# Retention and a multiplicative FFN on one core: weights converted 1024 columns at a time, w3 transposed by VectorE

## The chip, the cores and the metric

One core of a Trainium2 chip runs the whole program. The metric is the device time of one execution in microseconds (us). Short names: PE is TensorE (PEld its weight loads), DVE is VectorE, ACT is ScalarE, POOL is GpSimd, SP is the queue of SyncE, which issues most DMAs.

## What is computed

A retention block (8 batches, 8 heads, 576 positions, head size 64) gives x, which a feed-forward block takes. The weights arrive as 64-bit floats.

```python
scores = scale * np.matmul(q, k.transpose(0, 1, 3, 2))
ret = scores * Dmat[None, :, :, :]       # gamma[h] ** (i - j) for i >= j, else 0
x = np.matmul(ret, v)                    # then (B,H,S,D) -> (B*S, H*D) = (4608, 512)
a = x @ w1                               # 512 -> 1024
b = x @ w2                               # 512 -> 1024
h = a * b @ w3                           # 1024 -> 1024
out = h @ w_out                          # 1024 -> 512
```

## The kernel before, in words

**Chunks and units.** Tokens are taken in 4 pairs of batches. The retention runs in chunks of 128 positions (`load`, `scale`, `front`, `score`, `state`, `pv`): `load` fetches q, k and v from SP's queue, `front` transposes q and k on PE, `score` and `pv` are products, `state` carries the state along. The FFN works on a pair of batches and a third of the sequence: `up(i, n, fp)` makes one quarter fp of the 1024 inner columns of a and b by a Strassen scheme of seven products (L493), and multiplies a and b (L519). `down` multiplies by the matrix W = w3 @ w_out, which is made once on the chip.

**One `up`, in order.** Five PSUM tiles serve seven products; p1 and p5 are used twice. ACT copies p1 to c (L506), DVE adds S2 x T2 (the first addition, L498), S3 x T3 (the second), p5 = S1 x T1 (the third), A22 x -T4 (the fourth); then PE adds A12 x B21 to p1, ACT copies p1 again (L513), PE adds S4 x B22 to p5 (the seventh product; in the profile it is the group xT,wS), DVE adds p5 (the fifth addition) and multiplies the two halves of c (L519). There is one c. After each addition `convert(conv)` moves the conversion of the weights on by `conv` steps. The pool `acc` has seven PSUM banks.

**Conversion of the weights.** A 64-bit weight comes as two 32-bit words. Per block, DVE takes the exponent from the high word (tile e, L362) and the mantissa in two instructions (tile m, L366 and L369); ACT turns the exponent into a scale by two relus on e (L372, L373); DVE puts the sign on it (L383, the last reader of the loaded block) and multiplies m and e into the weight (L392, the output). `conversion()` is a generator: each `yield` is a step, and whoever calls `convert(n)` runs n steps, so the order of all engines is the order in which the program calls it. Between `begin_block` (L362 to L373) and `end_block` (L383, L392) of one block stands `begin_block` of the next. w1 and w2 come as four quarters, each of two matrices and two row halves: 16 blocks; when a quarter is whole, `strassen_weights` makes its sums S1 to S4 (L156). w_out is 8 blocks, w3 16, two for each 128 rows. A block is 512 columns, 512 KB as loaded; five buffers hold loaded blocks, so the load of block n+5 is issued when block n is done (L395, L396). DVE's transposes in 32x32 blocks are used elsewhere (`front_blocks`, L198).

**w3 @ w_out.** `w3_tr` transposes 128 rows of w3 on PE in eight 128x128 transposes (L438), and ACT copies them out of PSUM (L440). `w3_mm` multiplies them by w_out (L448; in the profile each product is two records) and ACT stores the sum (L451). The loop at L730 first runs the six `up`s of `todo`; with each it goes on with the conversion, and it interleaves `w3_tr` and `w3_mm`. When `todo` is empty, it runs `convert(10)` and PE has only this work until all 8 groups of rows are done. After it come one `up`, one `down` and the rest of retention and FFN.

**Memory.** The pools `raw` (loaded blocks, e, m) and the attention's pools share the right side of SBUF; `wst` (w_out, w3 and its transpose) takes the attention's place after L714. `open_attention` at L761 takes the place of `raw`, so the loads of the second half wait for the last block.

Of the kernel before, what the change touches and what calls it, by code (L numbers as in the profile page):

```python
# [8 lines left out]
F32 = mybir.dt.float32  # L9
I32 = mybir.dt.int32  # L10
U32 = mybir.dt.uint32
ALU = mybir.AluOpType
PSUM = bass.MemoryType.PSUM

# [24 lines left out]
def kernel(  # L39
# [13 lines left out]
    nc = tc.nc  # L53
    moe_w1, moe_w2, moe_w3, moe_w_out = (
        w.bitcast(I32).rearrange("r (c t) -> r c t", t=2) for w in (moe_w1, moe_w2, moe_w3, moe_w_out))
    B, H, S, D = q.shape
    DM = H * D
    DF = moe_w3.shape[0]
    CV = 512
    P = 128  # L60
    NP = H // 2
# [11 lines left out]
    KD = DM // P  # L73
    KF = DF // P
    QC = CV // 2
    NQ = DF // QC
    heads = [slice(j * D, (j + 1) * D) for j in range(2)]
# [10 lines left out]
    pools = {}  # L88
# [52 lines left out]

    halves = range(DF // CV)
    wA = [wp.tile([P, 2, KD, CV], F32, tag=f"wA{h}", name="wA") for h in halves]
# [10 lines left out]
    def strassen_weights(fp):  # L154
        def tt(out, in0, in1, op):
            nc.vector.tensor_tensor(out=A(fp, out), in0=A(fp, in0), in1=A(fp, in1), op=op)  # L156

        tt("S1", "A21", "A22", ALU.add)
        tt("S2", "S1", "A11", ALU.subtract)
        yield  # L160
        tt("S3", "A11", "A21", ALU.subtract)
        tt("S4", "A12", "S2", ALU.subtract)
        live["S", fp] = True
        yield

    BL = 32
# [142 lines left out]
    blocks = []  # L309
    for fp in range(NQ):  # L310
        for j, w in enumerate((moe_w1, moe_w2)):
            for r in range(2):
                blocks.append((("w12", fp, j, r), w))
    blocks += [(("wo", g), moe_w_out) for g in range(KF)]
    blocks += [(("w3", ft, g0), moe_w3) for ft in range(KF) for g0 in range(0, DF, CV)]
    at = {key: n for n, (key, _) in enumerate(blocks)}
    loaded, begun, converted, turned = [0], [0], [0], [0]

    def load_block():
        n = loaded[0]  # L320
        if n == len(blocks):
            return
        key, w = blocks[n]
        t = raw.tile([P, CV, 2], I32, tag="raw", name="raw", bufs=5)
        if key[0] == "w12":
            _, fp, _, r = key
            src = w[2 * r * P:2 * (r + 1) * P, fp * QC:(fp + 1) * QC, :]
            t2 = t.rearrange("p (c n) t -> p c n t", c=2)
            if r == 0:
                nc.sync.dma_start(t2, src.rearrange("(c p) n t -> p c n t", p=P))  # L330
            else:
                for half in range(2):
                    nc.sync.dma_start(t2[heads[half]],
                                      src.rearrange("(c a d) n t -> a d c n t", a=2, d=D)[1 - half])
        else:
            r, c0 = (key[1], 0) if key[0] == "wo" else key[1:]
            nc.sync.dma_start(t, w[r * P:(r + 1) * P, c0:c0 + CV, :])
        live["raw", n] = t
        loaded[0] += 1

    def converted_to(n):
        key, _ = blocks[n]
        if key[0] == "w12":
            _, fp, j, r = key
            return wA[fp // 2][:, j, 2 * r:2 * r + 2, fp % 2 * QC:fp % 2 * QC + QC]
        if key[0] == "wo":
            return live["wo"][:, key[1], :]
        _, ft, g0 = key
        if ("w3", ft) not in live:
            live["w3", ft] = pools["wst"].tile([P, DF], F32, tag="w3", name="w3")  # L350
        return live["w3", ft][:, g0:g0 + CV]

    def begin_block():
        n = begun[0]
        t = live["raw", n]
        lo, hi = t[:, :, 0], t[:, :, 1]
        e = raw.tile([P, CV], I32, tag="exp", name="e")
        m = raw.tile([P, CV], I32, tag="man", name="m")
        vec = nc.vector


        vec.tensor_scalar(out=e, in0=hi, scalar1=1, scalar2=21,  # L362
                          op0=ALU.logical_shift_left, op1=ALU.logical_shift_right)
        yield

        vec.tensor_scalar(out=m, in0=hi, scalar1=0x000FFFFF, scalar2=0x00100000,  # L366
                          op0=ALU.bitwise_and, op1=ALU.bitwise_or)
        yield
        vec.scalar_tensor_tensor(m.bitcast(F32), in0=lo.bitcast(U32), scalar=2.0 ** -32, in1=m,  # L369
                                 op0=ALU.mult, op1=ALU.add)  # L370
        relu = mybir.ActivationFunctionType.Relu
        nc.scalar.activation(e, e, relu, bias=lim[:, 0:1], scale=-1.0)  # L372
        nc.scalar.activation(e, e, relu, bias=lim[:, 1:2], scale=-2.0 ** 23)  # L373
        live["em", n] = e, m
        begun[0] += 1
        yield

    def end_block():
        n = converted[0]
        hi = live["raw", n][:, :, 1]  # L380
        e, m = live["em", n]
        vec = nc.vector
        vec.scalar_tensor_tensor(e, in0=hi, scalar=-(1 << 31), in1=e,  # L383
                                 op0=ALU.bitwise_and, op1=ALU.bitwise_or)
        yield
        key = blocks[n][0]
        while not (key[0] == "w12" or "wo" in live and (key[0] == "wo" or key[1] < turned[0] + 2)):
            yield "wait"
        out, m, e = converted_to(n), m.bitcast(F32), e.bitcast(F32)
        if key[0] == "w12":  # L390
            m, e = (x.rearrange("p (c n) -> p c n", c=2) for x in (m, e))
        vec.scalar_tensor_tensor(out, in0=m, scalar=2.0 ** -20, in1=e, op0=ALU.mult, op1=ALU.mult)  # L392
        converted[0] += 1

        if n >= 4:  # L395
            load_block()  # L396
        if key[0] == "w12" and key[1] > 0 and key[2:] == (1, 1):
            yield from strassen_weights(key[1])
        yield

    def conversion():


        yield from begin_block()
        while converted[0] < len(blocks):
            if begun[0] < len(blocks) and converted[0] not in (1, 2, 3):
                yield from begin_block()
            yield from end_block()
            if begun[0] == converted[0] < len(blocks):
                yield from begin_block()  # L410
# [11 lines left out]
    def convert(n):  # L422

        for _ in range(n):
            if go_on() is not None:
                return

    def convert_up_to(n):
        while converted[0] < n:
            assert go_on() is None  # L430


    def w3_tr(ft):
        t = pools["wst"].tile([P, KF, P], F32, tag="w3T", name="w3T")
        for i in range(0, KF, NP):
            tp = acc.tile([P, NP, P], F32, tag="acc", name="tp")
            for n in range(NP):
                nc.tensor.transpose(tp[:, n, :], live["w3", ft][:, (i + n) * P:(i + n + 1) * P],  # L438
                                    ident)
            nc.scalar.copy(t[:, i:i + NP, :], tp)  # L440
        live["w3T", ft] = t

    def w3_mm(ft, part):
        if part == 0:
            live["w3ps"] = acc.tile([P, DM], F32, tag="acc", name="ps")
        ps = live["w3ps"]
        for g in range(part * NP, part * NP + NP):
            nc.tensor.matmul(ps, live["w3T", ft][:, g, :], live["wo"][:, g, :],  # L448
                             start=(g == 0), stop=(g == KF - 1))
        if part == 1:  # L450
            nc.scalar.copy(live["w3o"][:, ft, :], ps)  # L451
# [24 lines left out]
    def up(i, n, fp, conv=0, tail=True):  # L476
# [43 lines left out]
        if tail:  # L520
            convert(conv)
# [142 lines left out]
    load_block()  # L664
# [8 lines left out]
    convert_up_to(3)  # L673
    load_block()
# [11 lines left out]
    up(0, 0, 0, conv=2, tail=False)  # L686
# [4 lines left out]
    convert(2)  # L691
# [4 lines left out]
    convert(5)  # L696
# [7 lines left out]
    up(0, 0, 1, conv=2)  # L704
# [5 lines left out]
    up(0, 1, 0, conv=2)  # L710
    pv(4)
    up(0, 1, 1, conv=2)
    up(0, 0, 2, conv=2)
# [15 lines left out]
    multiplied = 0  # L729
    while multiplied < KF:  # L730
        if todo:
            first = converted[0] < 4 * NQ
            up(*todo.pop(0), conv=2 if first else 1)
            convert(0 if first else 3)
        ft = multiplied
        begun_ft = ft < turned[0]
        if begun_ft:
            w3_mm(ft, 0)
        if turned[0] < KF and (not todo or converted[0] > at["w3", turned[0], DF - CV]):
            convert_up_to(at["w3", turned[0], DF - CV] + 1)  # L740
            w3_tr(turned[0])
            turned[0] += 1
        if begun_ft:
            w3_mm(ft, 1)
            multiplied += 1
        if not todo:
            convert(10)
# [138 lines left out]
```

## Time and profile before

| what | value |
|---|---|
| median of 3 runs | 872.9 us (872.61 to 873.29) |
| the profiled execution | 872.62 us |
| its span (first to last instruction) | 870.7 us |
| PE busy, all | 851.9 us |
| transposes of w3 on PE (L438) | 64, 273 ns each as recorded, 8 in 0.87 us in a row |
| products with w_out (L448) | 128 records, 593 ns each as recorded, 16 in 6.87 us in a row |
| DVE, instructions of the conversion | 40 of each kind, 128x512: L362 456, L366 420, L369 690, L383 693, L392 689 to 726 ns |
| ACT, relus | 40 of each, 723 and 722 ns |
| loads of weights | 512 KB and 256 KB, from SP |

How to read it: the profile is of one execution. A row of groups has the line, engine, operation, tiles out<-in, shape, count, busy time, mean of one, and the idle time of the engine before them with what ended it. A row of waits has engine, tile and line, what was waited for, and the total, the number and the longest of the waits. A row in the order of time has its start, its length, and in brackets the idle time before it. Matmuls are pipelined, so their recorded lengths overlap, and the time from start to start is what one costs.

### The profile page before, as it was taken

The page shows a single profiled execution, that of the slowest core. Times are in us where ns is not written, and L with a number is a line of the kernel's source. Part 1 is how long each engine was busy: PE and PEld are TensorE (multiplying, and loading weights), DVE is VectorE, ACT ScalarE, POOL GpSimd, SP SyncE. Part 2 cuts the span into 40 slices and gives each one's busy share as a digit, 9 for nine tenths or more (in the row PEclk, how much of TensorE's full clock was granted, in tenths as well). Part 3 has the DMA queues.
Part 4 walks back from the last instruction along what each step waited for, and adds up shares of the span by engine and source line. Part 5 has one row for each costly group of instructions (what it writes and reads, how often), then busy time and mean ns, then how long its engine had stood idle before and what let it go on. Part 6 is the DMA issues. An engine that isn't in the chain of part 4 may idle for free.

```text
span 870.7 us, 15305 instructions
## 1 busy us (share of the span) xinstructions
PE 851.9 (98%) x6373; PEld 779.0 (89%) x6373; DVE 458.3 (53%) x781; ACT 194.7 (22%) x390; POOL 111.8 (13%) x91
## 2 busy tenths in 40 slices
PE   5899999999999999999999999999999999999998
PEld 5899999645888999999999999999999999999996
DVE  4799998973543344643544544534543434334343
ACT  3676333553022221101111101111101100001000
POOL 3000020002001323201212030230300101000000
PEclk9999999999999999999999999999999999999999
DMA  9993443437035444515242335061300000000001
GB/s 194 218 223 107 98 99 104 139 120 108 1 77 118 114 63 82 95 28 93 49 84 44 55 68 96 27 104 34 59 25 25 2 25 1 25 24 1 25 1 49
DMA packets 187332, 63.20 MB, mean 73 GB/s; under 512 B 175480, under 2 KB 175480, under 8 KB 187264
## 3 DMA queue, kind: packets, MB, share of 16 engines
q1 hardware_dynamic: 154624, 54.07, 29.2%
q10 hardware_dynamic: 32640, 8.16, 4.9%
q8 instruction: 50, 0.82, 0.4%
q14 instruction: 18, 0.15, 0.1%
HBM read 52.76 MB, written 9.44 MB: 71 GB/s over the span
## 4 chain that ended last, share of the span: by engine, by line
PE 88%; DVE 3%; issue 1%; DMA 1%; ACT 1%; DVEq 0%; ACTq 0%; SPq 0%
PE up L493 46%; PE po L599 25%; PE ps L448 6%; PE sc L241 4%; PE xps L298 3%; PE xps L291 2%; PE tp L226 1%; PE st L263 1%; DVE c L498 1%; PE tp L438 1%; DVE e L383 0%; DMA raw<-in_moe_w_dram 0%; ACT e L372 0%; DVE ab L519 0%; DVE w L392 0%
## 5 line engine op out<-in xcount | busy, mean ns | idle before, releaser
L498 DVE TENSOR_TENSOR c<-up,c 128x384 f32<-128x384 f32 x240 | 133.2, 555 | 198.0 <-PE up L493 193.2
L493 PE MATMUL up<-xT,wA 128*128 128x192 f32 x1152 | 213.5, 329 | 1.0 <-ACT xT L303 1.0
L493 PEld LDWEIGHTS up<-xT,wA 128*128 128x128 f32 x1152 | 191.9, 191 | 3.6 <-ACT xT L303 1.2
L493 PE MATMUL up<-T,wS 128*128 128x192 f32 x768 | 141.1, 327 | 2.1 <-DVE T L467 2.1
L493 PEld LDWEIGHTS up<-T,wS 128*128 128x128 f32 x768 | 127.8, 191 | 2.4 <-issue 2.4
L599 PE MATMUL po<-w3o,ab 128*128 128x256 f32 x456 | 104.2, 381 | 0.3 <-ACT ot L621 0.3
L599 PEld LDWEIGHTS po<-w3o,ab 128*128 128x128 f32 x456 | 86.0, 190 | 12.1 <-ACT ot L621 0.7
L603 DVE TENSOR_TENSOR ot<-po,ot 128x256 f32<-128x256 f32 x90 | 38.1, 424 | 72.3 <-PE po L599 70.6
L513 ACT COPY c<-up 128x384 f32<-128x384 f32 x48 | 22.9, 477 | 226.3 <-PE up L493 222.0
L493 PE MATMUL up<-xT,wS 128*128 128x192 f32 x384 | 70.6, 327 | 0.6 <-DVE c L498 0.5
L493 PE MATMUL up<-T,wA 128*128 128x192 f32 x384 | 70.3, 326 | 0.0
L244 DVE TENSOR_TENSOR pm<-sc,mask 128x512 f32<-128x512 f32 (+1 forms) x80 | 45.5, 628 | 46.7 <-PE sc L241 46.5
L599 PE MATMUL po<-wB,forms 128*128 128x256 f32 x288 | 65.1, 379 | 0.0
L493 PEld LDWEIGHTS up<-xT,wS 128*128 128x128 f32 x384 | 63.6, 190 | 1.5 <-DVE c L498 1.5
L493 PEld LDWEIGHTS up<-T,wA 128*128 128x128 f32 x384 | 63.7, 190 | 0.0
L599 PEld LDWEIGHTS po<-wB,forms 128*128 128x128 f32 x288 | 54.8, 190 | 7.3
L212 POOL TENSOR_TENSOR ld_v<-ld_v,gk 128x1024 f32<-128x1024 f32 (+1 forms) x17 | 32.3, 1900 | 213.6 <-DMA ld_v<-in_v_dram 186.3
L448 PE MATMUL ps<-wo,w3T 128*128 128x512 f32 x128 | 56.4, 593 | 0.2 <-ACT w3T L440 0.2
L506 ACT COPY c<-up 128x384 f32<-128x384 f32 x48 | 22.8, 476 | 117.4 <-PE up L493 68.4
L467 POOL TENSOR_TENSOR T<-xT,T 128x384 f32<-128x384 f32 x20 | 20.9, 1043 | 217.1 <-PE up L493 215.4
L519 DVE TENSOR_TENSOR ab<-c 128x768 f32<-128x768 f32 x48 | 46.6, 972 | 3.8
L448 PEld LDWEIGHTS ps<-wo,w3T 128*128 128x128 f32 x128 | 23.7, 190 | 27.2 <-issue 26.7
(75 smaller groups left out, 817.8 us busy)
## 6 DMA issues: line engine op xcount, KB each, us to landing
raw<-in_moe_w_dram SPq DMA_DIRECT2D x24, 512.0 KB, 3.7
out_dram<-ot SPq DMA_DIRECT2D x24, 256.0 KB, 2.0
bl_q<-in_q_dram SPq DMA_DIRECT2D x136, 32.0 KB, 2.1
bl_k<-in_k_dram SPq DMA_DIRECT2D x136, 32.0 KB, 2.2
raw<-in_moe_w_dram SPq DMA_DIRECT2D x16, 256.0 KB, 6.1
ld_k<-in_k_dram SPq DMA_DIRECT2D x8, 512.0 KB, 7.1
ld_q<-in_q_dram SPq DMA_DIRECT2D x8, 512.0 KB, 8.2
ld_v<-in_v_dram SPq DMA_DIRECT2D x8, 512.0 KB, 7.4
```

The source lines that it names most:

```text
L212: nc.gpsimd.tensor_tensor(out=t, in0=t, in1=gam[:sz, c].unsqueeze(1).unsqueeze(3).to_broadcast([sz, 2, H, D]), op=ALU.mult)
L241: nc.tensor.matmul(sc[j][:sz, p, :sz], kT[hs, b, p, :sz], qT[hs, b, p, :sz], start=True, stop=True)
L244: nc.vector.tensor_mul(pm[:sz, b, j, :, :sz], sc[j][:sz, :, :sz], mask[:sz, :sz].unsqueeze(1).to_broadcast([sz, NP, sz]))
L298: nc.tensor.matmul(banks[r][heads[half], b, n, :sz], vs[:sz, b * H + 2 * p + j, :], pm[:sz, b, j, p, :sz], start=(c == 0 and m == 0), stop ...
L448: nc.tensor.matmul(ps, live["w3T", ft][:, g, :], live["wo"][:, g, :], start=(g == 0), stop=(g == KF - 1))
L493: nc.tensor.matmul(ps[:, w, :], a[:, w, r, :], b[:, r, :], start=(new and w == r == 0), stop=(w == r == 1), skip_group_check=True)
L498: nc.vector.tensor_add(c[:, to], ps, c[:, sb])
L506: nc.scalar.copy(c[:, 0], p1)
L513: nc.scalar.copy(c[:, 0], p1)
L519: nc.vector.tensor_mul(ab[:, 4 * fp:4 * fp + 4, :], c[:, :, 0, :], c[:, :, 1, :])
L599: nc.tensor.matmul(ps[nm], a[A][:, f, :], live["W"][B][:, f, :], start=(f == 0 and not on), stop=(f == NP - 1), skip_group_check=True)
L603: nc.vector.tensor_add(ot[:, to[0], to[1]], ps[nm], ot[:, sb[0], sb[1]])
```

## The change

Weights are converted in items of 1024 columns (CV; half of it is HC). The four first ones (the first quarter of w1 and w2, in halves) remain at 512. Of the loaded blocks there are two buffers of 1024 columns instead of five of 512, and one spare in an attention pool for the item ("w12", 1, 0). `begin_item` holds the exponent instruction and the relus, `mantissas` the two mantissa instructions, and `end_item` sign, output, for w3 a transpose on DVE, the next load and the sums. From item 4 on, `conversion` begins the next item, then makes the mantissas of this one, then ends it. w3 is loaded so that each 32 partitions hold 32-row blocks, in four DMAs per 128 rows; the rows of w_out are loaded in an order that fits. `w3_tr` and its copies go. The `up`s call the conversion with one step after each addition instead of two, and one at the end.

```diff
-        t = raw.tile([P, CV, 2], I32, tag="raw", name="raw", bufs=5)
...
+        if at_ == 0:
+            spare = key == ("w12", 1, 0)
+            live["raw", key] = (pools["fr"] if spare else raw).tile(
+                [P, CV, 2], I32, tag="raw", name="raw", bufs=1 if spare else 2)
...
+            src = moe_w3[r * P:(r + 1) * P].rearrange("(j r) (a f) t -> a r j f t", r=BL, f=FA)
+            t4 = t.rearrange("p (j f) t -> p j f t", f=FA)
+            for a in range(P // BL):
+                nc.sync.dma_start(t4[a * BL:(a + 1) * BL], src[a])
...
+    def begin_item(early=False):
...
         vec.tensor_scalar(out=e, in0=hi, scalar1=1, scalar2=21,
                           op0=ALU.logical_shift_left, op1=ALU.logical_shift_right)
+        relu = mybir.ActivationFunctionType.Relu
+        nc.scalar.activation(e, e, relu, bias=lim[:, 0:1], scale=-1.0)
+        nc.scalar.activation(e, e, relu, bias=lim[:, 1:2], scale=-2.0 ** 23)
+        begun[0] += 1
         yield
...
         vec.scalar_tensor_tensor(out, in0=m, scalar=2.0 ** -20, in1=e, op0=ALU.mult, op1=ALU.mult)
+        if kind == "w3":
+            yield
+            t = pools["wst"].tile([P, KF, P], F32, tag="w3T", name="w3T", bufs=3)
+            vec.transpose(t.rearrange("p i (j r) -> p j i r", r=BL), flat)
+            live["w3T", r] = t
         converted[0] += 1
 
-        if n >= 4:
+        if n >= 5:
             load_block()
-        if key[0] == "w12" and key[1] > 0 and key[2:] == (1, 1):
-            yield from strassen_weights(key[1])
+        if kind == "w12" and r > 0 and j == 1:
+            yield
+            yield from strassen_weights(r)
         yield
...
+        while converted[0] < len(items):
+            if begun[0] == converted[0]:
+                yield from begin_item()
+            first = converted[0] < 4
+            if first:
+                yield from mantissas()
+            elif begun[0] < len(items) and begun[0] == converted[0] + 1:
+                yield from begin_item()
+            if not first:
+                yield from mantissas()
+            yield from end_item()
...
-    def w3_tr(ft):
...
-    up(0, 0, 0, conv=2, tail=False)
+    up(0, 0, 0, conv=1)
...
-    while multiplied < KF:
+    while multiplied[0] < KF:
+        ft = multiplied[0]
         if todo:
...
+            up(*todo.pop(0), conv=1, tail=converted[0] < at["wo", 0, 0])
+        else:
+            convert_up_to(at["w3", ft, 0] + 1)
+        if converted[0] > at["w3", ft, 0]:
+            w3_mm(ft)
+            convert(1 if todo else 6)
```

In the part before the first `up`, one call of `load_block` after `load(2, "kqv")` and one after `convert_up_to(3)` go, so that items 0 to 6 are on their way there; the later ones are issued one each time an item ends.

## The prediction, made before the result was known

> **What bounds the kernel now.** I read the page's busy times and slices first, then the waits, then the order of time around the changed code. The profiled execution took 872.6 us with a span of 870.7 us, 0.3 us under the median of the runs shown (872.9); sums below start at 872.6.
>
> ```profile
> PE 851.9 (98%) x6373; PEld 779.0 (89%) x6373; DVE 458.3 (53%) x781; ACT 194.7 (22%) x390; POOL 111.8 (13%) x91
> DVE  4799998973543344643544544534543434334343
> ```
>
> PE is the bound as a whole. But in slices 2 to 7 (44 to 175 us), where all weights are converted, DVE is at 8 or 9 tenths too, and that is the stage that changes. What a late DVE costs there is seen in this row of PE's order of time:
>
> ```profile
> 111.31 1.57 PE L493 MATMUL up<-xT,wS 128*128 128x192 f32 x8 [0.53 <-DVE c L498]
> ```
>
> It is the seventh product of an `up`: it accumulates into p5, which the third addition of L498 has to read before. The seven products start 1.30 us apart, so from the end of p5's first product to the start of the seventh there are 2.6 us, 0.55 of them for the addition: DVE may be 2.0 us late there, and no more. The second limit is p1's second product, which needs the copy L506, which needs the multiplication L519 of the `up` before.
>
> The last stage of the conversion, w3 alone, runs from 160 to 223 us:
>
> ```profile
> 172.84 0.88 PE tp L438 x8
> 173.72 6.87 PE ps L448 x16
> 180.59 0.87 PE tp L438 x8
> ```
>
> Per 128 rows of w3, PE spends 6.87 us on products and 0.87 on transposes. DVE's order of time there shows one block of 512:
>
> ```profile
> 168.16 0.43 DVE L362 TENSOR_SCALAR e<-raw 128x512 int32<-128x512 int32 x1
> 168.50 0.42 DVE L366 TENSOR_SCALAR m<-raw 128x512 int32<-128x512 int32 x1
> 168.95 0.69 DVE L369 SCALAR_TENSOR_TENSOR m<-raw,m 128x512 f32<-128x512 uint32 x1
> 169.56 0.68 DVE L383 SCALAR_TENSOR_TENSOR e<-raw,e 128x512 int32<-128x512 int32 x1
> 170.28 0.69 DVE L392 SCALAR_TENSOR_TENSOR w<-m,e 128x512 f32<-128x512 f32 x1
> 171.01 0.44 DVE L362 TENSOR_SCALAR e<-raw 128x512 int32<-128x512 int32 x1
> ```
>
> From start to start 0.34, 0.45, 0.61, 0.72, 0.73: 2.85 us a block, 5.7 per 128 rows, under PE's 7.74. So PE bounds this stage now. The loads never show in it, because they run five blocks ahead. Two rows matter for what follows: what a load waits for, and how long it then takes (tile raw, 164 to 190 us):
>
> ```profile
> SPq L337 <- DVE e L383: 88.2, 23, 8.3
> DMA to landing us min/median/max: 3.5/3.6/3.7
> ```
>
> A load of 512 KB goes out when the sign instruction L383 of the block that held its buffer has ended, and lands 3.6 us later.
>
> **The change, part by part.**
>
> *Transposes off PE.* 8 x 0.87 = 7.0 us leave PE, and the wait before the second group (1.14 at 165.35 in PE's order of time): 8.1 together. ACT loses 16 copies (8.6 us), which lie beside other work.
>
> *Conversion at 1024.* L536 (1024 elements) took 1.214, L156 (512) 0.683: 0.53 per 512 more. So the three two-source instructions become 1.15, 1.25 and 1.25. TENSOR_SCALAR at 0.42 is already quicker; for it I bound the addition by 0.27 (half rate of the other, in proportion to 0.42 less a fixed 0.15) and 0.43 (doubling), and take 0.27, as 0.42 for 512 elements fits that rate: 0.6 and 0.7. Together 5.0 us per 1024 against 5.7. ACT: 128 elements took 0.392 (L210), 512 0.723 (L372), so 1024 take 1.17, two 2.35. The new transpose is like L198 (128x1024): 1.24. Per 128 rows of w3 DVE has 6.2 us of work against 6.87 on PE: by work alone it would fit.
>
> The row says that eight 128x128 transposes cost PE 0.87 us, 0.11 each, and DVE 1.24, 0.155 each. [...]
>
> *The buffers.* This decides. Before: five buffers of 512, and block n+5 is loaded when n is done. After: two of 1024 (the spare one serves one item), so item n+2 is loaded when the sign instruction a(n) has ended. And conversion() begins item n+2, its exponent instruction e, straight after the end of item n. DVE is in order: at e it waits for a transfer released just before, and everything behind stands, the additions of `up` included. On ACT the two relus wait for e, and behind them stands the copy L513.
>
> L, the time from release to landing for 1 MB, is not in the trace. Low: 512 KB in 3.6, and 512 KB more at the peak seen (420 GB/s in 0.4 us of 126 to 132 us): 4.8. High: three or four transfers issued up to 0.6 apart (L333), the last 1.8 after the first, with 4.4 for its own landing (64 to 68 us): 6.2. I take 5.1, near the low end, as all 8 loads from 164 us on agree within 0.2 us.
>
> [...]
>
> SP's queue: 32 issues for w3 instead of 16, at 0.33 to 0.6 each, 19 us at most in 75, on a queue that waits for DVE anyway. The 16 small loads of L721 (10.5 us of issue at 102.5) come to stand behind the load of item 11, at about 110, and are through by 121, before the next is due at 125; if they were not, each 1 us would be 1 us of that turn.
>
> *Where it bites, w3 stage.* From a(n) to a(n+1) stand L, then e 0.6, both mantissa instructions 0.7 and 1.15, and a 1.25: 5.1 + 3.7 = 8.8 us (8.5 to 9.9), against 6.87 on PE. DVE, waiting for DMA, becomes the bound.
>
> *Where it bites, `up` stage.* The steps of the generator, counted: 6 for item 4, then 5 for a first and 8 for a second half of w12 (four of them for sums and an empty one), 5 for w_out, 6 for w3. After 13 steps S1 is live, and the calls give 6, 6, 6, 6, then 5 per `up`. So e of item 12 falls behind the fourth addition of up(0,0,3), and so in each `up` after, one item per `up`. From a to a then: L 5.1, e 0.6, relus 2.35, L513 0.5, L519 0.95, the next L506 with its start 0.55, addition 0.5, mantissa 1.15, addition 0.5, a 1.25: 13.5 us. PE needs 9.1. Each such `up` costs 4.4; without ACT in the chain (the multiplication not waiting for L513) 11.1, and 2.0.
>
> *The start.* Items 0 to 3 remain 512 wide and in the same order; DMA is full there (212 to 237 GB/s to 70 us). e of item 5 now needs what was r6 and r7 (issued 31.6 to 32.9, landing after 8.2 to 8.9, to 41.8), before the third addition of up(0,0,0): that addition ends at 43.0, the seventh product moves from 42.1 to 43.05, 1 us. Item 6 likewise (lands about 53.5) puts S1 back by 1.3 more. Together 2.3; between 0 (covered by the shorter queue ahead of them) and 5.
>
> **The sum.** up(0,0,3) starts at 112.7 before. 2.3 from the start; in up(0,0,2) and up(0,1,2), e of items 10 and 11 waits 2.9 and nothing, and the third additions are 2.3 and 1.3 beyond the margin; 0.5 of before's own waits go: start at 112.7 + 5.4 = about 118. a(10) is 7.5 later (L506 has ended 4.1 after the start; addition 0.5, mantissa 1.15, addition 0.5, a 1.25): 125.5. Four turns of 13.5: a(14) at 179.5. Then addition, output, addition, transpose (0.5 + 1.3 + 0.5 + 1.2): 183, where the first w3 product starts, which started at 160.1. a(15): 179.5 + 8.8 + 1.0 for L519: 189.3. a(16) to a(20), five turns of 8.8: 233.3. Item 21 has no load behind it: output, transpose, mantissas, a, output, transpose take 8.1 to 241.4; the last but one product group ends at 235.8 + 6.9 = 242.7, the last at 249.6. Before: 222.7. So 26.9 us more, 872.6 + 26.9 = 899.5. The 8.1 us saved on PE are in this, and vanish: PE isn't the bound there. What follows is unchanged, since its attention loads, released at about 240, have 21 us of `up` and `down` before PE wants them.
>
> PE will stand idle some 2 us per turn. In the start 2.09 us idle (33.83) was followed by half speed (granted 0.83 in 30 to 40 us). A window at half speed, 3.4 us, would cost PE 1.7: 8.6 and 10.8 per turn, still under 8.8 and 13.5. I count nothing.
>
> **Rivals.**
> - *Hidden, faster.* Chance 0.14. One mechanism: the transfer lands before DVE reaches e. In the `up`s DVE then follows PE with 5 x 0.5 + 0.95 + 5.0 = 8.5 us of work per 9.1, and in the w3 stage 6.2 per 6.87. 872.6 - 8.1 = 864.5. For it: all landings were hidden till now. Against: DVE has only output and transpose, 2.5, between a and e in the w3 stage, PE is held up there from L = 6.87 - 3.7 = 3.2 on, and half the bytes took 3.6. It could only be if the release came from an earlier instruction than L383.
> - *Hidden in the `up`s alone.* Chance 0.14. PE's seven PSUM banks and the 2.0 us margin absorb the waits; the w3 stage still turns in 8.8. First product at 160, last end 66.6 later as above: 226.7, +4, with the start up to +6: 876 to 879.
> - *Within 0.2%.* Chance 0.04: the second rival with L near 4.4.
> - *The forecast.* 0.68: L from 4.8 to 6.2 over ten turns is -3 to +11, without ACT's part -10, the start -2 to +3, mantissa at twice the time +3: 885 to 916.
>
> **Numbers.** 899.5; the range goes from 876 (second rival) to 916. Slower by over 0.2% 0.82 (0.68 + 0.14), within 0.2% (about what can be told from no change) 0.04, faster 0.14.
>
> **What would show it.** A wait of DVE's e for DMA raw of some 2.5 us, about ten times, with turns of 8.8 between product groups in the w3 stage; PE idle before the xT,wS product behind L498 (before 0.5 us, after 2 to 4 per `up`); no L438; STREAM_TRANSPOSE x8 more at 1.2. I am wrong if e doesn't wait for DMA, if the release isn't the sign instruction, or if 1 MB lands in under 4 us.

## The result and the profile after

The changed kernel took 957.8 us (956.8 to 959.0, four runs) against 872.8 us on the same chip (872.3 to 873.3, four runs). The ratio is 1.0975, with a 95% interval of 1.0956 to 1.0994: slower by 85 us, where 27 were predicted. The profiled span is 955.1 us, 84.4 over before's. The two PE and DVE lines of the page that answer to those shown of before:

```profile
PE 867.5 (91%) x6309; PEld 782.7 (82%) x6309; DVE 458.3 (48%) x699; ACT 176.5 (18%) x338; POOL 112.0 (12%) x91
DVE  4787454446554633337435453444454333434343
```

DVE is busy for the same 458.3 us as before, but the slices from 96 to 310 us (the fifth to the thirteenth), where the conversion now lies, are at 4 to 6, where before's conversion had 8 and 9, and PE, 15.6 us busier in a span 84.4 us longer, has fallen from 98% to 91%. Nobody does much more work; somebody waits. The page's row of DVE's exponent instruction, with mean length and then the idle time before it, names the waiter:

```profile
L372 DVE TENSOR_SCALAR e<-raw 128x1024 int32<-128x1024 int32 (+1 forms) x22 | 15.4, 700 | 89.1 <-DMA raw<-in_moe_w_dram 45.5
```

89.1 us of waiting for loaded weights is about the size of the loss. Before's waits (total, number, longest) have 3.5 us of it:

```profile
DVE e L362 <- DMA raw<-in_moe_w_dram: 3.5, 2, 2.1
```

The waits of the changed kernel divide it between the matrices and show who stands behind:

```profile
DVE e L372 <- DMA raw<-in_moe_w_dram: 45.5, 12, 6.0
DVE e L372 <- DMA raw<-in_moe_w_out_dram: 43.6, 4, 11.9
...
PE up L520 <- ACT c L533: 31.4, 6, 10.4
...
PE up L520 <- DVE c L525: 19.6, 7, 11.0
PE ps L475 <- DVE w3T L423: 18.7, 7, 4.0
```

Four items of w_out cost as much as twelve of the others: 11 us each instead of 3.8. In DVE's order of time in the `up`s, one turn goes from sign instruction (L404, it frees the buffer) to sign instruction:

```profile
143.43 1.22 DVE L404 SCALAR_TENSOR_TENSOR e<-raw,e 128x1024 int32<-128x1024 int32 x1
158.62 0.69 DVE L372 TENSOR_SCALAR e<-raw 128x1024 int32<-128x1024 int32 x1 [11.91 <-DMA raw<-in_moe_w_out_dram]
165.71 1.21 DVE L404 SCALAR_TENSOR_TENSOR e<-raw,e 128x1024 int32<-128x1024 int32 x1
180.72 0.69 DVE L372 TENSOR_SCALAR e<-raw 128x1024 int32<-128x1024 int32 x1 [11.73 <-DMA raw<-in_moe_w_out_dram]
```

The sign instruction ends at 144.65, and the exponent of the item that takes its buffer begins at 158.62: 13.97 us for release and load, 22.3 for the turn. In the w3 stage:

```profile
242.68 1.23 DVE L404 SCALAR_TENSOR_TENSOR e<-raw,e 128x1024 int32<-128x1024 int32 x1
243.94 1.23 DVE L419 SCALAR_TENSOR_TENSOR w<-m,e 128x1024 f32<-128x1024 f32 x1
245.20 1.25 DVE L423 STREAM_TRANSPOSE w3T<-w 128x1024 f32<-128x1024 f32 x1
251.16 0.69 DVE L372 TENSOR_SCALAR e<-raw 128x1024 int32<-128x1024 int32 x1 [4.71 <-DMA raw<-in_moe_w_dram]
251.77 0.69 DVE L390 TENSOR_SCALAR m<-raw 128x1024 int32<-128x1024 int32 x1
252.49 1.23 DVE L393 SCALAR_TENSOR_TENSOR m<-raw,m 128x1024 f32<-128x1024 uint32 x1
253.63 1.22 DVE L404 SCALAR_TENSOR_TENSOR e<-raw,e 128x1024 int32<-128x1024 int32 x1
```

From the sign's end at 243.91 to the exponent at 251.16 there are 7.25 us, and the turn is 10.95. Why 14 us for one megabyte and 7 for another? Windows of 1 us (the last three columns are granted clock, mean busy share of the 16 DMA engines, GB/s), first during a load of w_out, then of w3:

```profile
154.00:155.00 1.00, 0.00 (x0) 0.00 (x0) 0.00 (x0) 0.00 (x0) 0.00 (x0) 1.00 0.24 98
...
247.00:248.00 1.00, 1.00 (x4) 0.42 (x3) 0.00 (x0) 0.00 (x0) 0.00 (x0) 1.00 1.03 219
248.00:249.00 1.00, 1.00 (x4) 0.52 (x3) 0.00 (x0) 0.00 (x0) 0.00 (x0) 1.00 1.05 209
```

In the load of w_out the share is 0.24, at 98 GB/s. In the load of w3 it is 1.03 and 1.05, and still only 219 and 209 GB/s move, where before's peak was 420.

### The profile page after: what moved, and what is told of

It is laid out like the page before. It is cut to its first block, busy times and chain, and to the rows that moved or that the text cites. A ratio compares the mean times of both kernels' runs of the same rounds, so it can differ in the third digit from the quotient of the medians.

```text
span 955.1 us, 15045 instructions
## 1 busy us (share of the span) xinstructions
PE 867.5 (91%) x6309; PEld 782.7 (82%) x6309; DVE 458.3 (48%) x699; ACT 176.5 (18%) x338; POOL 112.0 (12%) x91
## 4 chain that ended last, share of the span: by engine, by line
PE 72%; DMA 14%; DVE 7%; SPq 3%; ACT 2%; issue 2%; POOL 0%; DVEq 0%; ACTq 0%
PE up L520 38%; PE po L625 22%; DMA raw<-in_moe_w_dram 7%; DMA raw<-in_moe_w_out_dram 6%; PE sc L242 3%; PE xps L299 3%; PE ps L475 2%; PE xps L292 1%; DVE e L404 1%; PE st L264 1%; DVE c L525 1%; PE tp L227 1%; DVE m L393 1%; SPq L357 1%; DVE e L372 1%
## 5 line engine op out<-in xcount | busy, mean ns | idle before, releaser
L520 PE MATMUL up<-xT,wA 128*128 128x192 f32 x1152 | 220.4, 336 | 32.6 <-ACT c L533 30.7
L520 PEld LDWEIGHTS up<-xT,wA 128*128 128x128 f32 x1152 | 197.5, 196 | 37.1 <-ACT c L533 32.2
L520 PE MATMUL up<-xT,wS 128*128 128x192 f32 x384 | 74.0, 337 | 19.6 <-DVE c L525 19.6
L520 PEld LDWEIGHTS up<-xT,wS 128*128 128x128 f32 x384 | 65.7, 196 | 22.3 <-DVE c L525 22.3
L475 PE MATMUL ps<-wo,w3T 128*128 128x512 f32 x128 | 65.1, 668 | 18.7 <-DVE w3T L423 18.7
L475 PEld LDWEIGHTS ps<-wo,w3T 128*128 128x128 f32 x128 | 26.8, 215 | 56.5 <-issue 39.6
L245 DVE TENSOR_TENSOR pm<-sc,mask 128x512 f32<-128x512 f32 (+1 forms) x80 | 45.5, 627 | 46.2 <-PE sc L242 46.1
L540 ACT COPY c<-up 128x384 f32<-128x384 f32 x48 | 22.8, 475 | 216.4 <-PE up L520 216.4
L372 DVE TENSOR_SCALAR e<-raw 128x1024 int32<-128x1024 int32 (+1 forms) x22 | 15.4, 700 | 89.1 <-DMA raw<-in_moe_w_dram 45.5
L546 DVE TENSOR_TENSOR ab<-c 128x768 f32<-128x768 f32 x48 | 49.0, 1020 | 12.5 <-ACT c L540 8.7
L375 ACT ACTIVATE e<-e,lim 128x1024 int32<-128x1024 int32 (+1 forms) x22 | 23.6, 1073 | 155.6 <-DVE e L372 155.6
```

The costliest lines, as they stand in the source:

```text
L245: nc.vector.tensor_mul(pm[:sz, b, j, :, :sz], sc[j][:sz, :, :sz], mask[:sz, :sz].unsqueeze(1).to_broadcast([sz, NP, sz]))
L372: vec.tensor_scalar(out=e, in0=hi, scalar1=1, scalar2=21, op0=ALU.logical_shift_left, op1=ALU.logical_shift_right)
L520: nc.tensor.matmul(ps[:, w, :], a[:, w, r, :], b[:, r, :], start=(new and w == r == 0), stop=(w == r == 1), skip_group_check=True)
L546: nc.vector.tensor_mul(ab[:, 4 * fp:4 * fp + 4, :], c[:, :, 0, :], c[:, :, 1, :])
```

## The experiments

**Theory**: each turn holds the time L from release to landing, as predicted, but L is not 5.1. The change also reshaped the loads: w_out comes in a pattern whose slowest dimension has 4 members, w3 in four DMAs of 32 partitions each. **Rivals**: the longer instructions, or PE at half clock after its waits, cost the extra time; or DVE's transpose in itself does.

A time given without a number of runs is that of one run; the kernel before took 871.7 to 874.7 us in all of its runs.

**e1_wo16**: each DMA of w_out becomes four, one per 32 partitions.

```diff
-                nc.sync.dma_start(t4[:, c], src[r + c])
+                for a in range(P // BL):
+                    nc.sync.dma_start(t4[a * BL:(a + 1) * BL, c], src[r + c, a])
```

> The changed kernel with each 1024-column item of w_out loaded in 8 transfers of 32 partitions instead of 2 of 128 partitions (whose outermost dimension has 4 members). Theory (each turn of the conversion holds the whole time from the sign instruction to the landing, and for w_out that is 13.9 us because only a quarter of the DMA engines work, share 0.24 to 0.27): the share rises to near 1, the time to 6 to 8 us, the four waits of e for w_out (43.6 us) fall by 6 to 7 each, 928 to 935 us. Rival A (1 MB simply takes that long from memory): no change, 956 to 959. Rival B (the waits cover for other work; PE at half clock and DVE's long instructions set the time): the waits shrink but under 10 us are gained, above 948.

926.7 us (before, on that chip: 871.8): 31 less than the changed kernel, 1 under the range. Its waits:

```profile
DVE e L373 <- DMA raw<-in_moe_w_dram: 47.1, 13, 6.0
...
DVE e L373 <- DMA raw<-in_moe_w_out_dram: 13.6, 3, 4.7
```

w_out's waits fall from 43.6 to 13.6, by the whole gain; those of the other matrices stay. So the pattern of w_out alone cost some 30 us against loads of 32 partitions.

**e2_w3plain**: w3 in one DMA of whole rows, 8 KB per partition. The arrangement by 32 rows is left out, so the products are of other rows.

```diff
...
-            for a in range(P // BL):
-                nc.sync.dma_start(t4[a * BL:(a + 1) * BL], src[a])
+            nc.sync.dma_start(t, moe_w3[r * P:(r + 1) * P])
```

> The changed kernel with 128 rows of w3 loaded in one transfer of whole rows; this leaves out the arrangement in 32-row blocks, so the product is made of other elements of w3. Theory (the shape of the transfers decides, four of 32 partitions one after the other run at some 210 GB/s): from sign to landing 5.0 to 5.5 us instead of 7.3, turns in the w3 stage 8.7 to 9.2 instead of 11.1, and two turns in the ups shorter by 2: 937 to 944 us. Rival A (1 MB takes 7.3 in any shape): 956 to 959. Rival B: turns stay, above 950.

935.2 us (before: 871.8), 2 under the range. One of its windows, during a load of w3:

```profile
236.00:237.00 1.00, 1.00 (x3) 0.47 (x3) 0.00 (x0) 0.00 (x0) 0.00 (x0) 1.00 1.02 434
```

At the same share of 1 the same bytes move at 434 GB/s instead of 209 to 219. From the sign's end to the exponent it takes 5.2 us (233.14 to 238.31) instead of 7.25, in the other turns of the stage 4.7 to 4.9, and the turns are 8.4 to 8.9.

This run changes two things at once: 128 partitions a DMA instead of 32, and pieces of a row of 8 KB instead of 2 KB. The loads of w_out in e1 tell them apart, with pieces of 4 KB into 32 partitions:

```profile
132.00:133.00 1.00, 1.00 (x8) 1.00 (x7) 0.00 (x0) 0.00 (x0) 0.70 (x1) 1.00 0.99 197
133.00:134.00 1.00, 1.00 (x8) 1.00 (x7) 0.00 (x0) 0.00 (x0) 0.00 (x0) 1.00 1.04 275
```

Before's loads of w3 have pieces of 4 KB too, over 128 partitions:

```profile
127.60:128.00 0.40, 0.40 (x5) 0.40 (x4) 0.40 (x2) 0.38 (x1) 0.00 (x0) 1.00 1.05 420
```

In these windows, with pieces of the same 4 KB, loads into 32 partitions moved 197 and 275 GB/s at shares of 0.99 and 1.04, and loads over 128 moved 420 at 1.05: most of the difference goes with the number of partitions. Whether pieces of 2 KB add to it, these runs don't separate.

**e10_both_plain**: both matrices in DMAs of whole rows; both arrangements are left out.

```diff
...
-                nc.sync.dma_start(t4[:, c], src[r + c])
+                nc.sync.dma_start(t4[:, c], moe_w_out[(r + c) * P:(r + c + 1) * P])
...
+            nc.sync.dma_start(t, moe_w3[r * P:(r + 1) * P])
```

> The changed kernel, two buffers and the exponent first, with w3 and w_out loaded in transfers of whole rows over 128 partitions as in the kernel before; this leaves out the arrangement of both, so the product is another one. Theory (the prediction's sum was right but for the transfers' length, 5.1 us assumed): turns of 8.6 in the w3 stage and 13.5 in the ups, 895 to 903 us, the 899.5 of the prediction among them. Rival (a further cost that the prediction left out): above 908.

899.7 us; the prediction said 899.5. DVE's order of time:

```profile
138.42 1.21 DVE L400 SCALAR_TENSOR_TENSOR e<-raw,e 128x1024 int32<-128x1024 int32 x1
144.55 0.69 DVE L368 TENSOR_SCALAR e<-raw 128x1024 int32<-128x1024 int32 x1 [2.85 <-DMA raw<-in_moe_w_out_dram]
151.65 1.22 DVE L400 SCALAR_TENSOR_TENSOR e<-raw,e 128x1024 int32<-128x1024 int32 x1
```

L is 4.92 here, the turn 13.23. With loads over 128 partitions the prediction's sum holds, and so do its marks, within 1.4 us (table below). So the two shapes, with the waits and the half clock that follow from them, are the difference. The instructions are as long as in the changed kernel, so the first rival falls as to them.

**e3_elate**: the exponent of the next item goes behind the mantissas of this one, so that DVE reaches its wait later.

```diff
-            elif begun[0] < len(items) and begun[0] == converted[0] + 1:
-                yield from begin_item()
-            if not first:
-                yield from mantissas()
+            else:
+                yield from mantissas()
+                if begun[0] < len(items) and begun[0] == converted[0] + 1:
+                    yield from begin_item()
```

> The changed kernel with the exponent of the next item placed behind the mantissas of the present one instead of ahead of them; all loads as they are. Theory (the transfer is waited for where the exponent stands in DVE's and ACT's order): w3 turns 11.1 - 1.85 = 9.2; in the ups the wait no longer stands ahead of the copy L540, a turn is the transfer plus 2.4 instead of plus 8.4: 905 to 920 us. Rival A (the transfers alone set the pace, wherever they are waited for): turns shorter by less than 1, above 945. Rival B: above 945.

915.7 us (before: 871.8). Waits for w_out 26.9 instead of 43.6, for the others 22.8 instead of 45.5; w3 turns of 9.1 to 9.4. **e8_wo16_elate** is e1 and e3 together:

> The changed kernel with two buffers, w_out in 8 transfers (e1) and the exponent of the next item behind the mantissas (e3). Theory (the terms add: e3 kept 27 us of waits for w_out, which e1's transfers of about 7 us bring to near 0; w3's turns stay at 9.2): 886 to 894 us. Rival (the two gains overlap): above 900.

892.2 us. Order alone brings 42 us, order and w_out's pattern 66 of the 85: what is left of L after the work that DVE can put in front of it still counts.

**e4_three**: three buffers of 1024, loads three items ahead. To make room the spare goes, the w3 weights are written into the mantissa tile, w3T has two buffers, and the pool xp1 is opened after the weights' pool is closed.

```diff
-            spare = key == ("w12", 1, 0)
-            live["raw", key] = (pools["fr"] if spare else raw).tile(
-                [P, CV, 2], I32, tag="raw", name="raw", bufs=1 if spare else 2)
+            live["raw", key] = raw.tile([P, CV, 2], I32, tag="raw", name="raw", bufs=3)
...
-            flat = pools["wst"].tile([P, CV], F32, tag="w3", name="w3", bufs=1)
+            flat = m
...
-        if n >= 5:
+        if n >= 4:
```

> The changed kernel with three buffers of 1024 columns and loads three items ahead (no spare buffer; to make room the product of w3 goes into the mantissa's tile, two tiles of the transpose instead of three, and one pool is opened later). All transfers as they are. Theory (two buffers are the cause): the transfer is spread over two turns, (13.9 + 8.4) / 2 = 11.2 in the w_out turns, w3 turns at PE's 6.9, 870 to 885 us. Rival A (shapes of the transfers alone, DMA is the bound): 925 or more. Rival B (PE at half clock, DVE's long instructions): above 930.

890.5 us (before: 871.8), a miss by 5.5. One long wait for w_out remains, and SP's queue shows a part of why:

```profile
111.33 22.31 SPq L741 DMA_DIRECT2D gqs<-decay_q_dram  x16
...
152.37 0.69 DVE L370 TENSOR_SCALAR e<-raw 128x1024 int32<-128x1024 int32 x1 [12.58 <-DMA raw<-in_moe_w_out_dram]
```

The 16 small loads of gqs held the queue for 10.5 us before; behind w_out's loads in the pattern with 4 members (share 0.24 to 0.26 in e4's windows from 146 to 152 us) they hold it for 22.3. The buffer of the next load is free at 127.10, and it is issued only at 133.75: 6.7 us of the 12.6. From there to the exponent it takes 18.6 us instead of 14; the first load of w3, issued at 137.75, is under way beside it. That this is what slows it isn't shown.

**e5_three_wo16**: e4 and e1 together, so that neither buffers nor w_out's pattern can hold DVE.

> The kernel of e4 (three buffers) with w_out in 8 transfers of 32 partitions as in e1. Theory (in e4 one wait of 12.6 us for w_out is left, behind 16 small loads that stand 22 us in SP's queue while four DMA engines carry w_out): it goes, 874 to 880 us; what is left over the kernel before is the start, +3 to +5 at the first product of up(0,0,2), and the saved transposes, -7. Rival (conversion at 1024 costs by itself, whatever the loads): 886 or more.

874.4 us over 10 runs (before: 873.8), ratio 1.0015 (1.0006 to 1.0024). The slowdown is all but gone, with every instruction 1024 wide and every transpose on DVE: neither the widths nor the transposes cost the 85 us. The 8 us of saved transposes don't show, since the start is 3.8 us later than before's and PE's order of time has, in five `up`s, rows such as

```profile
135.11 1.57 PE L519 MATMUL up<-xT,wS 128*128 128x192 f32 x8 [1.60 <-DVE c L524]
```

**e9_three_wo16_elate**: e5 with the order of e3.

> The kernel of e5 (three buffers, w_out in 8 transfers) with the exponent of the next item behind the mantissas as in e3. Theory (in e5 no transfer is waited for after 66 us; what is left of the loss is 1 us in each of five ups, as the relus of the next item stand ahead of the copy L539 on ACT, and 3.8 us at the start): the five times 1 us go, and part of the start's waits for items 4 to 6, 866 to 870 us, faster than the kernel before. Rival (DVE's work of 8.5 us per up and the additions late by long instructions are the cause, not the order): 873 to 876 as e5.

873.1 us over 12 runs, ratio 0.9995 (0.9985 to 1.0004): a miss, no difference from before. These waits go, all but one, and the w3 stage ends 2.9 us earlier than in e5. But up(0,0,2) starts 2.2 later, though at 66 us e9 was still 1.2 ahead. ACT's order of time and PE's show the place:

```profile
67.56 1.15 ACT L375 ACTIVATE e<-e,lim 128x1024 int32<-128x1024 int32 x1
68.61 2.43 ACT L211 ACTIVATE ld_q<-ld_q,gq 128x128 f32<-128x128 f32 x8
```

```profile
69.34 0.33 PE L227 MATMUL tp<-ident,ld_q 128*128 128x128 f32 x1 [1.15 <-ACT ld_q L211]
```

The relus of the later exponent stand ahead of the scaling of q, for which PE's transposes wait; from 72 to 76 us PE's granted clock is then 0.68, in e5 1.00.

**e7_before_wo4**: the kernel before, with only w_out's pattern changed. The rows of w_out come in another order, so the products differ.

```diff
...
+            if key[0] == "wo":
+                nc.sync.dma_start(t, w.rearrange("(a i x) n t -> i a x n t", i=KF, x=32)[r])
```

> The kernel before with w_out alone loaded in the changed kernel's order, one transfer of 512 KB whose outermost dimension has 4 members; this permutes the rows of w_out, so the product is another one. Theory (four engines carry it, and five buffers cover it): landing 6.5 to 7.5 us instead of 3.5, DMA share 0.25 at these loads, time within 3 us of the kernel before. Rival (such a load costs time in itself): 880 or more. Rival (the order of rows in memory is not what made it slow): landing 3.5 to 4.5.

878.5 us (before: 873.8), a miss by 2. A window of one such load shows a share near a quarter again (0.26, at 102 GB/s), and PE's order of time what came through:

```profile
88.00:89.00 1.00, 1.00 (x8) 1.00 (x8) 0.96 (x3) 0.43 (x1) 0.00 (x0) 1.00 0.26 102
...
134.23 2.93 PE L496 MATMUL up<-xT,wS 128*128 128x192 f32 x8 [4.00 <-DVE c L501]
```

Five buffers hide the same pattern but for one wait of 4 us, behind gqs's loads (18.3 us in the queue). A slow pattern costs some 30 us with two buffers and 5 with five. The trace holds no time to landing for these loads.

**e6_before_dvetr**: the kernel before with DVE's transposes alone: blocks of 512, five buffers, w3 and w_out in DMAs of 32 partitions.

```diff
+            vec.transpose(live["w3T", key[1]].rearrange("p i (j r) -> p j i r", r=BL)[:, 2 * h:2 * h + 2],
+                          live["flat"])
...
+        if converted[0] > at["w3", ft, DF - CV]:
+            w3_mm(ft)
+            if not todo:
+                convert(12)
```

> The kernel before with only one part of the change: w3 loaded by 32-row blocks and transposed on DVE, in blocks of 512 columns with five buffers, w_out in the order that fits by 4 transfers of 32 partitions a block. Theory (the transposes are worth 7 to 8 us once no load is waited for): 864 to 868 us. Rival (DVE then has 5.7 + 1.4 = 7.1 us per 128 rows against 6.9 on PE, and the slower loads of 32 partitions show): 870 to 876.

924.6 us over 4 runs, ratio 1.0584 (1.0562 to 1.0607): far off, and neither theory's. Its waits and ACT's order of time:

```profile
DVE e L389 <- ACT e L379: 41.7, 8, 8.0
PE ps L449 <- DVE w3T L404: 36.4, 8, 5.7
```

```profile
193.81 0.59 ACT L451 COPY w3o<-ps 128x512 f32<-128x512 f32 x1 [10.96 <-PE ps L449]
194.29 0.72 ACT L378 ACTIVATE e<-e,lim 128x512 int32<-128x512 int32 x1
```

No load is among these waits. The conversion stands behind the products in program order, so ACT's relus stand behind the copy of the sum, which waits for PE, which waits for DVE, which waits for the relus. **e11_before_dvetr2** converts the next 128 rows ahead of the products, and runs three steps instead of four after each later `up`; against e6:

```diff
-            convert(0 if first else 4)
+            convert(0 if first else 3)
...
-            convert_up_to(at["w3", ft, DF - CV] + 1)
+            convert_up_to(at["w3", min(ft + 1, KF - 1), DF - CV] + 1)
+            convert(4)
...
-            if not todo:
-                convert(12)
```

> The kernel of e6 (the kernel before with w3 transposed on DVE, 512 columns, five buffers) with the blocks of the next 128 rows converted ahead of the product of these, so that their relus stand ahead of the copy of the product on ACT. Theory (e6's w3 stage waited 6.6 us per 128 rows for relus queued behind that copy, not for transposes or loads): w3 turns 7.1 (DVE) instead of 13.7, 866 to 873 us. Rival (transposing on DVE at 512 columns costs by itself): above 890.

868.2 us over 4 runs against 873.7, ratio 0.9939 (0.9925 to 0.9954): 0.6% faster than before. So the transposes on DVE go with a gain of 5.5 us where the widths and the five buffers stay; with them change the shapes of the loads and the order of conversion and products, and no run gives each its share. The second rival, that they cost time in themselves, falls. PE's order of time, first products of the w3 stage:

```profile
159.34 7.03 PE L449 MATMUL ps<-wo,w3T 128*128 128x512 f32 x16
168.03 48.74 PE L449 MATMUL ps<-wo,w3T 128*128 128x512 f32 x112 [1.66 <-DVE w3T L404]
```

The marks of all versions in us, from PE's order of time:

| mark | before | predicted | after | e10 | e5 | e9 | e11 |
|---|---|---|---|---|---|---|---|
| up(0,0,2) starts | 93.7 | 96.0 | 97.1 | 97.4 | 97.5 | 99.7 | 94.5 |
| up(0,0,3) starts | 112.7 | 118 | 129.0 | 118.6 | 115.9 | 119.5 | 113.5 |
| first w3 product | 160.1 | 183 | 224.5 | 183.3 | 168.9 | 165.3 | 159.3 |
| w3 stage ends | 222.6 | 249.6 | 306.9 | 248.6 | 224.4 | 221.5 | 216.6 |
| span | 870.7 | 897.6 | 955.1 | 897.7 | 872.5 | 870.6 | 865.7 |

(Predicted: the span is before's plus the 26.9; up(0,0,2) is before's start plus the 2.3.)

## Why the prediction was right in direction and wrong in size

- **The mechanism: right.** With two buffers and the exponent ahead of DVE's other work, every load's full time stands in a turn. In the five turns inside the w3 stage and the four in the `up`s that it counted, the formulas hold to 0.1: L + 3.7 (7.25 + 3.7 = 10.95, measured 10.95), L + 8.4 (13.97 + 8.4 = 22.4, measured 22.3).
- **L, the failed step.** "I take 5.1", between 4.8 and 6.2. For whole rows it is 4.7 to 5.2; for the loads that the change issues it is 13.8 to 14.9 (w_out) and 7.2 to 8.1 (w3). The working looked at bytes and number of DMAs. Its lower bound comes from loads over 128 partitions, its upper one from the landing of 256 KB into 64 partitions (L333) and the times of issue; neither asks what the diff's `rearrange` does to the rate. A warning stood in the prediction's own rows: DMA "full" at 212 to 237 GB/s up to 70 us, beside a peak of 420. No run here says what lowers the rate there.
- **With the measured L the marks follow.** The exponent of item 10 waits 11.8 us, not 2.9 (11 us more at up(0,0,3), the start's 1.1 included). From there to the end of the sign instruction of item 10 it is 15.7, not 7.5 (8), as the exponent of item 11 waits 8.2 and not nothing. Four turns take 76.5, not 54 (22). The w3 stage takes 82.4, not 66.6 (16). Together 57 of the 58 us that were missing, some 2.5 of them by the half clock that came with the waits.
- **What the shapes do.** The windows show a share of 0.24 at 98 GB/s for w_out, in a pattern whose slowest dimension has 4 members, and of 1.03 at 219 GB/s for w3, in DMAs of 32 partitions; whole rows over 128 partitions moved 434 GB/s at a share of 1.02 (e2). The share is a mean over the 16 engines: that only four of them work on w_out, as the expectations of e1, e5 and e7 have it, is the author's estimate from a share of 0.24 to 0.27. Which engines carry a load, and what halves the rate at a share of 1, isn't shown.
- **Conversion at 1024: right.** From start to start 0.61, 0.72, 1.14, 1.26 and 1.26, 4.99 together against 5.0; the transpose 1.25 against 1.24; a relu 1.15 against 1.17.
- **Transposes off PE: right.** They are gone, and invisible in the changed kernel, as predicted, since PE waits there for DVE. Where PE is the bound, the w3 stage falls from 63.8 us, the transposes ahead of its first product included, to 55.5 (e5) and 57.3 (e11): by 8.3 and 6.5, against 8.1.
- **The start: 2.3 predicted, 3.4 measured**, inside its 0 to 5. Three exponents wait 0.94, 2.77 and 1.71 for the first wide loads.
- **gqs's loads.** Predicted through by 121 with 10.5 us of issue; they hold the queue for 19.4 us, to 141.3, ahead of the load of item 12, which is released at 144.65. That load lost nothing by it; the load of item 11, under way beside them, took 14.9 us where the other three of w_out took 13.8 to 14.0. In e4 they held a load back by 6.7 us.
- **Half clock: nothing counted, about 2.5 us measured.** The granted clock is 0.50 from 110 to 120 and from 160 to 170 us, in and behind waits of PE of 11.0 and 10.4 us; the prediction's window of 3.4 us is that of before's start (0.97, 0.50, 0.50, 0.50 and 0.82 from 34 to 39 us, by 1 us). In the turns it costs nothing, as predicted: w3 products of 7.10 and of 9.60 us stand in turns of the same 11 us. But the product at 116 us delays the fifth addition, and with it the sign instruction of item 9, by 0.8 us, and the last two groups, with nothing left to wait for, take 15.5 us to the next `up` (granted clock 0.50 from 292 to 295 us) where those of e10 take 13.8 (1.00). First the changed kernel's, then e10's:

```profile
291.33 15.70 PE L475 MATMUL ps<-wo,w3T 128*128 128x512 f32 x32 [1.91 <-DVE w3T L423]
```

```profile
234.74 14.00 PE L471 MATMUL ps<-wo,w3T 128*128 128x512 f32 x32 [1.43 <-DVE w3T L419]
```

- **The rivals.** Hidden, and hidden in the `up`s, fall: L is far above 3.2, and the exponents wait in both stages. "Within 0.2%" took L near 4.4 for 1 MB, which no run shows; the least measured are 4.7 to 5.2, for whole rows (e2, e10). The range ended at 916 because L ended at 6.2.

## What to carry to other kernels

Before fewer and larger buffers, work out for each load the time from release to landing, in the shape in which it will be issued; what doesn't fit under the work between release and first use is paid in every turn, by everything queued behind on that engine (here DVE waited 8.2 to 11.9 us in each turn of w_out, and 4.7 to 4.9 in each inside the w3 stage). A load's time is not its bytes (1 MB took 4.7 to 5.2 us in whole rows, 13.8 to 14.9 in w_out's pattern in the changed kernel): read from the diff how many members the slowest dimension has (4 went with 98 GB/s) and how many partitions one DMA writes (32 went with 219, 128 with 434), and read the DMA share beside GB/s. An instruction that waits for a load belongs as late in its engine's program as its data allows (e3, on DVE: 42 us less), and never behind something that waits for its own result (e6, on ACT: 924.6 us, e11 868.2).

## What the runs showed that was not expected

- One megabyte took 13.97 us (4 members outermost, share 0.24, 98 GB/s), 7.25 us (four DMAs of 32 partitions, share 1.03, 219 GB/s) and 4.7 to 5.2 us (whole rows, up to 434 GB/s). A share of 1 did not mean full rate.
- Sixteen small loads took 10.5 us of SP's queue before, 18.3 to 22.3 us (e7, the changed kernel, e4) behind loads of w_out at a share near 0.25, and 10.7 in e10, behind whole rows.
- What stays open: why one of the w3 loads issued during the `up`s took 8.1 us, when the other seven took 7.2 to 7.5. No run tells that apart.
